# A gated recurrence and two MoE matmuls: first chunks of four batches at once, and all later loads uncast on GpSimd's queue

## The chip, the cores and the metric

The kernel runs on one core of one Trainium2 chip. The metric is the device time of one execution in microseconds (us), as a median over several runs. The kernel before takes 190.9 us (190.21 to 191.94, three runs). A verdict of faster or slower needs a difference of over 2%. The span of a profile is a little shorter than the time of its run, by 1.6 to 3 us here.

The engines are PE (TensorE matmul), PEld (its weight loads), DVE (VectorE), ACT (ScalarE), POOL (GpSimd) and SP (SyncE). Each works through its own instructions in a fixed order: in this kernel every instruction is pinned in the order that a small planner in the kernel works out beforehand.

## The reference

```
state = zeros(B, H, D, D)                       # B, H, S, D = 4, 8, 768, 48
for t in range(S):
    state = alpha[:, :, t, :, None] * state + einsum('bhd,bhe->bhde', k[:, :, t], v[:, :, t])
    y[:, :, t] = einsum('bhd,bhde->bhe', q[:, :, t], state)
x = y.transpose(0, 2, 1, 3).reshape(3072, 384)
h = x @ w_in                                    # 384 x 2048
out = (max(h, 0) ** 2) @ w_out                  # 2048 x 384
```

The recurrence is done in 24 chunks of 128 tokens, six for each batch. Each chunk has a cumulative decay (logarithm, triangular matmul, exponentials), scores, a mask and a value product. The state goes from a chunk to the next of the same batch, and starts at zero in each batch. The finished tokens (x tiles) feed two large matmuls, MoE1 and MoE2, which are most of PE's work.

## The kernel before

The first four chunks belong to batch 0. Alpha and q of these come in rows of four tokens ("slots"), k and v chunk by chunk. Later chunks follow batch by batch. Alpha, q and k go over SyncE's queue (all but seven early loads, which GpSimd issues uncast); v goes over GpSimd's queue and is cast to bf16 by the transfer itself, after a one-column copy that holds it back until the previous k has landed.

```
srcs = [("at", alpha), ("qt", q), ("kt", k), ("vt", v)]
slot_srcs = {n: a[0, :, 0:4 * P, :].rearrange("h (p j) d -> p h (j d)", j=4) for n, a in srcs}
srcs = [(n, a.rearrange("b h (c p) d -> b c p h d", p=P)) for n, a in srcs]
...
def load_tile(nm):
    if nm == "vt":
        return loads.tile([P, H, D], BF16, name=nm, bufs=LBV)      # LBV = 6
    return loads.tile([P, H, D], FP32, name=nm)                    # LB = 5
...
        def ld(nm=nm, src=src):                                    # in add_loads
            if nm not in d:
                d[nm] = load_tile(nm)
            if nm == "vt" and after:
                pin(nc.gpsimd.tensor_copy(d[nm][:, 0, 0:1], after["kt"][:, 0, 0:1]))
            pin((nc.gpsimd if pool or nm == "vt" else nc.sync).dma_start(out=d[nm], in_=src[b, c]))
...
ld_at = [load_slots("at", i * H // 2, (i + 1) * H // 2) for i in range(2)]
ld_qt = [load_slots("qt", i * H // 2, (i + 1) * H // 2) for i in range(2)]
for s in range(NJ):
    add_loads(s, ("kt", "vt"), pool=s == NJ - 1)
four_slots(ld_at, ld_qt)
for s in range(NJ):
    add_chunk(s)
for x in "iiiioo4oo5":                   # i, o: parts of w_in and w_out, by GpSimd
    ...
for s in range(6, NT):
    add_loads(s, after=C[s - 1])
    add_chunk(s)
```

The planner (`plan.run`) sorts all operations by a modelled start, and they are then issued in that order on each engine.

## Time and profile before

| what | before |
|---|---|
| time, median | 190.9 us |
| span of the profile | 189.4 us |
| first MoE matmul starts | 22.50 us |
| last matmul ends | 186.3 us |
| PE busy | 180.2 us (95%) |
| POOL busy | 42.2 us (22%) |
| DMA packets | 94,280 |

The prediction below shows the stretches, the chain and the timeline that matter. One more view belongs here, because it is the one that answers directly after a change: PE's waits, by whom it waited for, in us in total, times and the longest. The largest of the kernel before:

```profile
PE bank L229 <- DVE kI_s L474: 2.1, 2, 1.4
```

And the stretch from the first MoE matmul to 60 us as one row (length, busy us of PE, PEld, DVE, ACT and POOL with their instructions, granted PE clock, DMA share, GB/s):

```profile
22.50:60.00 37.50, 37.33 (x448) 29.29 (x449) 26.38 (x56) 26.20 (x63) 10.52 (x17) 0.97 1.21 183
```

PE rests 0.17 us of these 37.50, and POOL is busy for little more than a quarter.

### The profile page before, as it was taken

Reading aid. Unit: us, or ns where it says so; the run is one execution under the profiler, and the core shown is the slowest. Engines: PE = TensorE matmul, PEld = TensorE weight load, DVE = VectorE, ACT = ScalarE, POOL = GpSimd, SP = SyncE. Lnnn points to the kernel's source line nnn. Section 1 sums busy time; section 2 is a strip of 40 time slices with the busy share of each in tenths; the row PEclk is TensorE's granted clock in tenths of the full one; section 3 lists DMA queues with packets and bytes.
Section 4 is the critical chain, followed back from the end, with each engine's and each line's share of the span. In section 5 each row is a group of like instructions: output and inputs, shape, how many; then the busy total and the mean of one; then the engine's idle time right before and its main releaser. Section 6 shows DMA issues by size and latency. Waiting matters only on the chain.

```text
span 189.4 us, 5215 instructions
## 1 busy us (share of the span) xinstructions
PE 180.2 (95%) x1999; PEld 137.1 (72%) x1999; DVE 132.3 (70%) x335; ACT 126.7 (67%) x346; POOL 42.2 (22%) x78
## 2 busy tenths in 40 slices
PE   7864999999999999999999999999999999999993
PEld 2553778866878887777777787787787787777773
DVE  3167946754899795897886886886886886944411
ACT  3763459926778886678588588488588586565630
POOL 8967335023122233222021031041000000000000
PEclk9998589999999999999999999999999999999999
DMA  5999999899999999999959739739011011011112
GB/s 177 238 165 203 204 223 211 125 183 147 183 191 185 206 180 173 201 153 188 218 130 142 166 84 124 170 87 126 0 45 43 3 42 45 6 37 45 42 42 83
DMA packets 94280, 24.71 MB, mean 130 GB/s; under 512 B 85216, under 2 KB 93920, under 8 KB 94256
## 3 DMA queue, kind: packets, MB, share of 16 engines
q1 hardware_dynamic: 64992, 17.45, 44.8%
q0 software_dynamic: 29120, 6.88, 37.5%
q8 instruction: 15, 0.25, 0.6%
q14 instruction: 9, 0.07, 0.1%
q10 hardware_dynamic: 144, 0.05, 0.1%
HBM read 25.17 MB, written 4.72 MB: 158 GB/s over the span
## 4 chain that ended last, share of the span: by engine, by line
PE 87%; DMA 5%; SPq 3%; ACT 1%; DVE 1%; issue 1%; ACTq 0%; DVEq 0%
PE bank L226 78%; PE bank L229 7%; DMA kt<-in_k_dram 5%; PE st L226 2%; SPq L339 2%; SPq L319 1%; ACT r L668 1%; DVE st L578 1%; DVE sm L533 1%; ACT sb L583 0%; ACT xn L220 0%; DVE ob L736 0%; ACT ob L736 0%; ACT L_s L442 0%; DVE kI_s L474 0%
## 5 line engine op out<-in xcount | busy, mean ns | idle before, releaser
L668 ACT ACTIVATE r<-bank 128x256 bf16<-128x256 f32 (+1 forms) x160 | 64.7, 429 | 29.6 <-PE bank L226 28.2
L226 PE MATMUL bank<-xT_big,w_in_b 128*128 128x256 bf16 (+1 forms) x624 | 80.0, 266 | 0.1
L226 PE MATMUL bank<-w_out_b,gT 128*128 128x384 bf16 (+1 forms) x400 | 74.7, 320 | 0.0
L226 PEld LDWEIGHTS <-w_in_b 128*128 128x128 bf16 x624 | 53.8, 98 | 9.7 <-issue 0.5
L675 DVE TENSOR_TENSOR gT<-r 128x256 bf16<-128x256 bf16 (+1 forms) x160 | 47.6, 315 | 16.0 <-ACT r L668 14.4
L226 PEld LDWEIGHTS <-gT 128*128 128x128 bf16 x400 | 37.9, 98 | 15.8
L533 DVE TENSOR_TENSOR sm<-bank,utri_b 128x512 bf16<-128x512 f32 x40 | 25.3, 683 | 2.6 <-PE bank L226 2.5
L339 POOL DMA_DIRECT2D vt<-in_v_dram x24 | 21.3, 888 | 7.9 <-POOL vt L338 6.1
L338 POOL CAST vt<-kt 128x1 bf16<-128x1 f32 x18 | 4.7, 263 | 64.6 <-PE bank L226 41.8
L471 DVE TENSOR_TENSOR qA_s<-qt,A 128x384 bf16<-128x384 f32 x20 | 11.1, 556 | 9.5 <-ACT A L458 8.6
L218 DVE COPY qkT<-bank 128x1024 bf16<-128x1024 bf16 x20 | 13.8, 688 | 4.9 <-PE bank L229 4.9
L474 DVE TENSOR_TENSOR kI_s<-kt,Ainv 128x384 bf16<-128x384 f32 x24 | 13.3, 556 | 3.1 <-DMA kt<-in_k_dram 2.6
L709 ACT COPY ob<-bank 128x384 f32<-128x384 f32 x21 | 10.1, 480 | 8.1 <-PE bank L226 8.1
L226 PEld LDWEIGHTS <-qkT 64*128 64x128 bf16 (+1 forms) x260 | 10.4, 97 | 5.9 <-issue 2.5
L220 ACT CAST xn<-bank 128x384 bf16<-128x384 f32 x23 | 10.9, 480 | 4.2 <-PE bank L226 3.8
L583 ACT CAST sb<-st 128x384 bf16<-128x384 f32 x20 | 9.6, 478 | 5.7 <-DVE st L578 5.7
L458 ACT ACTIVATE A<-bank 128x384 bf16<-128x384 f32 x20 | 9.9, 496 | 2.4 <-PE bank L226 2.4
L229 PE MATMUL bank<-ident_bf,kI_s 128*128 128x128 bf16 x96 | 9.5, 223 | 2.1 <-DVE kI_s L474 2.1
L578 DVE TENSOR_TENSOR st<-st,ae_s 128x384 f32<-128x384 f32 x20 | 11.1, 556 | 0.0
L442 ACT ACTIVATE L_s<-at 128x384 bf16<-128x384 f32 x20 | 10.4, 521 | 0.0
L462 ACT ACTIVATE Ainv<-bank 128x384 bf16<-128x384 f32 x20 | 10.2, 510 | 0.0
L229 PE MATMUL bank<-ident_bf,qA_s 128*128 128x128 bf16 x96 | 9.3, 219 | 0.8 <-DVE qA_s L407 0.7
(78 smaller groups left out, 162.1 us busy)
## 6 DMA issues: line engine op xcount, KB each, us to landing
out_dram<-ob SPq DMA_DIRECT2D x23, 192.0 KB, 2.7
kt<-in_k_dram SPq DMA_DIRECT2D x21, 192.0 KB, 5.3
at<-in_alpha_dram SPq DMA_DIRECT2D x18, 192.0 KB, 4.8
qt<-in_q_dram SPq DMA_DIRECT2D x18, 192.0 KB, 4.7
vt<-in_v_dram POOLq DMA_DIRECT2D x24, 96.0 KB, 5.6
w_in_b<-in_moe_w_in_dram POOLq DMA_DIRECT2D x4, 384.0 KB, 11.0
w_out_b<-in_moe_w_out_dram POOLq DMA_DIRECT2D x4, 384.0 KB, 12.3
slot_at<-in_alpha_dram SPq DMA_DIRECT2D x2, 384.0 KB, 3.6
```

The source lines that it names most:

```text
L218: pin(nc.vector.tensor_copy(out, in_))
L220: pin(nc.scalar.copy(out, in_))
L226: pin(nc.tensor.matmul(*a, **kw))
L229: pin(nc.tensor.transpose(*a))
L339: pin((nc.gpsimd if pool or nm == "vt" else nc.sync).dma_start(out=d[nm], in_=src[b, c]))
L442: pin(nc.scalar.activation(L[:, :, 0:D], d["at"], AF.Ln))
L471: pin(nc.vector.tensor_mul(qA[:, :, 0:D], d["qt"], d["A"]))
L474: pin((nc.vector if mk.eng == "DVE" else nc.gpsimd).tensor_mul(kI[:, :, 0:D], d["kt"], d["Ai"]))
L533: pin(nc.vector.tensor_mul(d["sm"][:, hh], d["sc"][hh], (utri_p if first else utri_b).to_broadcast([P, NP, P])))
L578: pin(nc.vector.tensor_mul(st4, st4, bcast(ae, D)))
L668: pin(nc.scalar.activation(box["r"], box["ph"], AF.Relu))
L675: pin(nc.vector.tensor_mul(gT[g][:, f0:f0 + nf, 0:n], box["r"], box["r"]))
```

## The change

Its intent: the first chunk of every batch needs no incoming state, so the first chunks of all four batches are done together, by head pairs, with alpha, q and k in rows of four tokens, in parts of 96 KB. After that the chunks go batch by batch. All later loads, alpha, q, k and v, are issued by GpSimd without a cast, and a copy on GpSimd casts v to bf16. This gives fewer and larger packets and frees SyncE. A hold makes w_in wait for v's first part.

```diff
-    LB = 5
-    LBV = 6
+    LB = 4
+    SEQ = [(b, 0) for b in range(B)] + [(b, c) for b in range(B) for c in range(1, NCH)]
...
+    def load(s, names=("at", "qt", "kt", "vt")):
+        b, c = SEQ[s]
+        for nm in names:
+            def ld(nm=nm):
+                C[s][nm] = loads.tile([P, H, D], FP32, name=nm)
+                pin(nc.gpsimd.dma_start(out=C[s][nm], in_=srcs[nm][c, :, b * H:(b + 1) * H]))
+            C[s]["ld_" + nm] = pool_dma(LDS, X_ISSUE, ld, C[s - LB]["use_" + nm] if s - LB >= B else None)
...
+        def e_vb():
+            d["vb"] = work.tile([P, H, D], BF16, name="vb", bufs=4)
+            pin(nc.gpsimd.tensor_copy(d["vb"], d["vt"]))
+        if first:
+            vb = d["vb_op"]
+        else:
+            vb = d["use_vt"] = add("POOL", 0.52, e_vb, d["ld_vt"], C[s - 4].get("end") if s >= 8 else None, prio=-60.0)
...
+    ld_at = [load_part("at", h, nc.sync if h % 2 == 0 else nc.scalar, 0.9 + 0.45 * (h // 2)) for h in range(H)]
+    w_gate[:] = [bmask]
+    ld_qt = [load_part("qt", h, nc.sync, 2.7 + 0.45 * h) for h in range(B)]
+    ld_kt = [load_part_pool("kt", h) for h in range(B)]
+    ld_qt += [load_part("qt", h, nc.sync, 2.7 + 0.45 * h) for h in range(B, H)]
+    ld_kt += [load_part("kt", h, nc.sync, 4.5 + 0.45 * h) for h in range(B, H)]
...
+    ld_vt = [load_v(j, 8.1 + 0.45 * j) for j in range(NJ)]
+    def hold():
+        pin(nc.gpsimd.tensor_copy(w_in_b[0:PQ, 0, 0:1], v_0[0:PQ, 0, 0, 0:1]))
+    w_gate[:] = [add("POOL", 0.1, hold, ld_vt[0], utri, prio=-70.0)]
+    first_chunks(ld_at, ld_qt, ld_kt, ld_vt)
...
-    for s in range(6, NT):
-        add_loads(s, after=C[s - 1])
-        add_chunk(s)
+    order = ["i", "i", "i", "i", 4, "o", "o", "o", "o"]
+    for x in order + list(range(5, NT)):
+        ...
+            load(x)
+            if c == 1:
+                add_keys(b, 20.0 if b == 0 else 30.0)
+                add_state(b)
+            add_chunk(x)
```

Cut from the diff: the new masks, the first chunks' decay, transposes and copies by head pairs, the table of priorities, and the output of the first tiles in four-token rows.

## The prediction

> **What bounds the kernel now.** I read the page first, then busy time by stretch, then the chain of waits in order of time, then the timeline of the ramp. The page says PE 95% busy; by stretch:
>
> ```profile
> 0.00:6.00 6.00, 4.28 (x19) 1.87 (x20) 1.83 (x10) 2.83 (x3) 5.28 (x22) 1.00 0.67 193
> 6.00:14.00 8.00, 6.28 (x84) 4.17 (x83) 3.75 (x8) 5.63 (x15) 6.63 (x9) 1.00 1.65 195
> 14.00:22.50 8.50, 6.06 (x76) 4.14 (x71) 6.87 (x13) 3.89 (x10) 4.54 (x6) 0.73 1.28 202
> 22.50:36.00 13.50, 13.50 (x129) 11.35 (x130) 8.23 (x19) 10.12 (x20) 4.80 (x6) 0.92 1.32 208
> 36.00:60.00 24.00, 23.83 (x322) 17.94 (x320) 18.15 (x38) 16.08 (x44) 5.73 (x11) 1.00 1.15 170
> 60.00:160.00 100.00, 100.00 (x1137) 77.76 (x1135) 80.84 (x210) 74.75 (x222) 15.27 (x26) 1.00 0.80 122
> ```
>
> Columns: stretch, length, then PE, weight load, DVE, ACT, POOL busy (instructions), granted clock, DMA share, GB/s. From 22.5 us on PE never rests: that part is PE work alone, and a faster load there buys nothing. Only the ramp before 22.5 us, the lowered clock around it and a few gaps before 60 us can be gained. The chain of waits says what the ramp waits for:
>
> ```profile
> 3.47 2.81 SPq L339
> 6.33 9.01 DMA kt<-in_k_dram
> 22.50 15.27 PE bank L226 x139
> ```
>
> A key load is issued late, because SyncE's queue is held for 2.81 us, and takes 9.01 us. The timeline shows whom it holds, and what the first MoE matmul then waits for:
>
> ```profile
> 15.36 0.56 DVE L474 TENSOR_TENSOR kI_s<-kt,Ainv 128x384 bf16<-128x384 f32 x1 [1.69 <-DMA kt<-in_k_dram]
> 15.84 0.56 DVE L578 TENSOR_TENSOR st<-st,ae_s 128x384 f32<-128x384 f32 x1
> 16.31 1.28 DVE L533 TENSOR_TENSOR sm<-bank,utri_p 128x512 bf16<-128x512 f32 x2
> 22.50 0.80 PE L226 MATMUL bank<-xT_big,w_in_b 128*128 128x256 bf16 x3
> ```
>
> DVE runs in order, so the late key holds the state and mask multiplies behind it, and these hold the first tiles of x. MoE starts at 22.50 us; the last matmul ends at 186.3.
>
> **What the Trainium skill says.**
> 1. "DMA: Bandwidth & Descriptors", Specifications: transfers under 512 B miss line rate. The trace agrees: while the slot loads of alpha (768 B runs) flow alone, between 3 and 5 us, the row shows 330 to 390 GB/s; in 60 to 80 us, with runs of 192 B, 185.
> 2. The same page, "SWDGE vs HWDGE vs iDMA": GpSimd's descriptors are grouped into packets of up to 4 KB. The trace fits, for uncast loads only. Of the 29,120 packets on q0, the 24 cast loads of v take 24 x 1024 = 24,576 and the eight weight loads 4 x 384 + 4 x 512 = 3,584; 960 remain for seven uncast loads that have 7,168 runs of 192 B.
> 3. "SBUF — State Buffer", "SBUF: two separate sides": a GpSimd operation and a DVE operation with two SBUF inputs exclude each other for the whole instruction. The casts on GpSimd that the change adds could meet the squares. In this trace GpSimd's one-column casts take 0.18 to 0.57 us, which may be that; nothing here settles it.
> 4. "TensorE: Matmul & The Clock Gate", Part 1: PE's clock halves after a quiet window and returns after about 3.4 us of activity. The page of the kernel before shows the clock at 5 tenths in the slice around 19 to 24 us, after the sparse ramp.
>
> **The change part by part.**
>
> *Later loads, all on GpSimd's queue, uncast.* Before, in 60 to 80 us, a hardware packet cost 0.882 x 16 x 20 us / 14,256 = 19.8 ns and a packet of the casting v load 0.473 x 16 x 20 / 5,200 = 29.1 ns, so a cast load costs more DMA time than an uncast one of twice the written bytes. The change frees DMA time there, but PE is at 100.00 of 100: worth 0 us. Its cost: 4 issues x 0.88 us + one cast of some 0.5 us (estimate) = 4.0 us of GpSimd per chunk; PE takes about 164/24 = 6.8 us per chunk. It fits.
>
> *PE's work.* I counted matmuls in both orders and priced them by start-to-start times of the timeline (MoE1 66 in 7.22 us = 0.109; MoE2 8 in 1.30 = 0.163; transpose 8 in 0.45 = 0.056; state or inter-chunk 4 in 0.17 = 0.042; value product about 0.025). After the first MoE matmul the changed kernel has 16 more transposes (keys turned back, +0.90), 16 more state products (+0.68), 4 more inter-chunk products (+0.17), 3 fewer transposes of xn (-0.17), 8 fewer value products (-0.20): **+1.4 us**. Less lies before it (first chunks without states), but there PE waits anyway.
>
> *The ramp.* Four first chunks of four batches need no state, and all of alpha, q and k now comes in runs of 768 B. Step by step:
> - Alpha: 384 KB issued at 0.81 was in at 4.13. A part has 96 KB; less 0.8 us of transfer at 350 GB/s it lands about 2.5 us after issue. SyncE issues one per 0.46 us. ACT issues the other four; if its table load (0.80 to 2.08) holds that queue, heads 0 to 3 are in at about 5.1 us, if not, at 3.8. Half each.
> - ACT then does 4 logarithms x 0.52 + 8 exponentials x 0.50 + 2 small x 0.18 + one copy 0.59 = 7.0 us before the last inverse decay: 12.1 or 10.8.
> - Key multiply 0.56, transposes 0.3, copy 0.59, first scores and latency about 1: masks start near 14.6 or 13.3. All scores wait for all transposed heads.
> - DVE has six masks x 0.68, a copy 0.36, a mask 0.68, a copy 0.36 = 5.5 us before the first two x tiles are complete: 20.1 or 18.8, plus some 0.5 of latencies and stretch: 20.6 or 19.3. Middle **20.0, so -2.5 us** against 22.50.
> - Does v come in time? SyncE has issued 16 parts by about 8.2 us; 768 KB of v at 185 GB/s takes 4.2, with w_in beside it: landed about 15.5. Then four casts at 0.5 us: 16 to 18 us. The first value product needs its masks at about 16: close, not behind.
> - w_in is held back for v's first part, landing near 12: issued 12 to 15 us, the first part in at about 17.5, where it also is now (issue 8.85, plus 8.7). In time.
>
> *The sum.* -2.5 + 1.4 = -1.1 us, and a further -0.2 because the chunk loads are no longer pacing 40 to 60 us: 190.9 - 1.3 = **189.6 us**. The gain is small because the work in front of PE moves from waiting for k to a dense ACT and DVE line that ends only 2.5 us sooner.
>
> **The rivals.**
> - *ACT becomes the bound after the ramp.* From the start of MoE to the end of the first MoE1 rounds its order holds 20 relus x 0.60, 3 key copies, 2 chunks of decay work (2 x 1.9), 2 state casts, one xn: about 19 us, against about 19 us of PE work there (MoE1 of five tiles 13, MoE2 2.6, chunk 4 and keys 3). Three PSUM banks feed ACT, so lateness goes to PE at once. For: ACT had 10.12 of 13.50 us there before. It would give back 1 to 3 us: 190.6 to 192.
> - *GpSimd's line becomes the bound.* It does masks, four k parts, a hold, weights, casts and all loads in order. If v lands after 18 us, casts, w_out and chunk 4 all slip: up to +3 us, about 192.5. For: q0 waits in the trace for earlier transfers (1.0 to 1.6 us before several issues). Against: merged packets, and chunk 4 is first needed about 6 us into MoE.
> - *The clock.* Before, MoE's first 2.5 us ran at half clock, about 1.25 us lost. If the changed ramp keeps PE warm, 1.2 us more are gained: 188.4. Sparse transposes between 9 and 14 us speak against it.
> - *Everything goes well*: ACT's queue isn't held, the clock is up, and the gaps go (matmuls counted after 22.5 are 160.4 us of the 163.8 spent): 19.3 + 161.8 + 3.1 of tail + 1.6 between span and time = about 186.
>
> **Range and chances.** The start of MoE is uncertain by 1.3 us either way, what ACT or GpSimd gives back by 0 to 3, the clock by 1.2. The range is 186.5 to 192.4. Faster by 2% means under 187.1, which needs nearly all of the good case: 0.18. Slower by 2% means over 194.7, which needs loads late for several chunks: 0.07. Within 2%: 0.75.
>
> **What would show it.** Right: the wait for k gone from the chain, its place taken by ACT's exponentials and DVE's masks; first MoE matmul between 19 and 21 us; PE at 100 of 100 from 60 to 160 us as before; GpSimd busy near 50%; q0 with few, large packets. Wrong: PE gaps after 22 us that end with a relu (ACT), or with a load or value cast (GpSimd); a first MoE matmul after 22 or before 18.5 us; or a vanished dip of the clock, which would make the gain larger than the ramp's.

## The result, and the profile after

| what | before | after |
|---|---|---|
| time, median (four runs each) | 190.73 us | 199.57 us (198.55 to 199.91) |
| ratio of the fast runs | 1 | 1.0446, 95% interval 1.0383 to 1.0509 |
| span of the profile | 189.4 us | 196.7 us |
| first MoE matmul starts | 22.50 us | 21.65 us |
| last matmul ends | 186.3 us | 193.6 us |
| PE busy | 180.2 us (95%) | 181.5 us (92%) |
| POOL busy | 42.2 us (22%) | 95.2 us (48%) |
| DMA packets | 94,280 | 20,026 |

The changed kernel is slower by 4.5%. Here and below a ratio is the mean time of one kernel's fast runs over the mean of the other's fast runs of the same rounds, so it is not quite the ratio of the medians.

MoE starts 0.85 us earlier, and all of the loss comes after. PE's largest wait and the same stretch as before, now of the changed kernel, show where:

```profile
PE st L205 <- POOL vb L495: 5.1, 2, 4.2
```

```profile
22.50:60.00 37.50, 32.00 (x356) 24.58 (x354) 21.75 (x47) 22.20 (x53) 30.20 (x38) 0.90 1.09 217
```

The first row is a wait that did not exist before: a state matmul (`st`) waits for the cast of v (`vb`, L495) on GpSimd, twice, once for 4.2 us. The last row answers the one shown of before: PE rests 5.50 us of 37.50 in place of 0.17, and its clock is 0.90 in place of 0.97. GpSimd is busy three times as long.

GpSimd's timeline between 31 and 49 us (start, length, engine, line, operation, and in brackets the idle time before it and its releaser):

```profile
31.77 0.88 POOL L444 DMA_DIRECT2D vt<-in_v_dram  x1 [1.47 <-DMA vt<-in_v_dram]
32.65 0.52 POOL L495 CAST vb<-vt 128x384 bf16<-128x384 f32 x1
33.09 0.88 POOL L444 DMA_DIRECT2D at<-in_alpha_dram  x1
34.98 0.88 POOL L444 DMA_DIRECT2D qt<-in_q_dram  x1 [1.00 <-DMA w_out_b<-in_moe_w_out_dram]
36.92 0.88 POOL L444 DMA_DIRECT2D kt<-in_k_dram  x1 [1.06 <-DMA w_out_b<-in_moe_w_out_dram]
39.47 0.89 POOL L444 DMA_DIRECT2D vt<-in_v_dram  x1 [1.67 <-DMA w_out_b<-in_moe_w_out_dram]
...
47.46 0.88 POOL L444 DMA_DIRECT2D at<-in_alpha_dram  x1
48.34 0.52 POOL L495 CAST vb<-vt 128x384 bf16<-128x384 f32 x1
```

The load of v for chunk 5 is issued at 31.77 us. Its cast comes at 48.34 us. The row at 32.65 us is the cast of chunk 4; between the two casts stand thirteen issues, the loads of chunks 6, 7 and 8 and the alpha of chunk 9. That is 13 x 0.88 = 11.4 us of issuing and another 3.7 us in which three of these issues waited for parts of w_out to land. The order is fixed, so a cast of 0.52 us stands behind issues whose data nobody needs yet. Its own data had landed some 6 us before (at 42.23 us by the trace; put earlier, in the first experiment, the same cast waited for them to 42.24 us), and PE wanted the result at 44.7 us. A likely reason for the order lies in the planner, in the kernel above: it counts 0.88 us for an issue and knows nothing of these waits for earlier transfers, so its times for GpSimd and for the landing need not be those of the chip. No run tests that.

PE's side of it, and then the two stretches around it in the form of the rows above:

```profile
48.91 0.48 PE L205 MATMUL st<-vb,kI_s 128*128 128x96 bf16 x4 [4.21 <-POOL vb L495]
```

```profile
44.53:48.91 4.38, 0.17 (x3) 0.00 (x1) 0.24 (x1) 0.00 (x0) 4.26 (x7) 0.75 1.04 220
48.91:53.48 4.57, 4.57 (x38) 2.84 (x37) 2.79 (x5) 1.47 (x5) 4.57 (x6) 0.50 1.03 217
```

PE, DVE and ACT all stop for 4.4 us while only GpSimd issues loads. When the cast is done, PE works at half clock (0.50) for another 4.6 us. From 60 us on PE is full again in both kernels.

How the loss adds up: by the prediction's count and prices of matmuls (an estimate), PE has 160.4 us of work from the first MoE matmul on before, and 161.8 us after; it took 163.8 us before (22.50 to 186.3) and 171.95 us after (21.65 to 193.6). What is left over, 3.4 us before and 10.2 us after, is put down to gaps and clock: -0.85 (ramp) + 1.4 (more work) + 6.8 (gaps and clock) = +7.3 us, which is the difference of the spans, 196.7 - 189.4.

The ramp gained 0.85 us and not 2.5. Three engines' rows of the changed kernel, ACT, DVE and PE, and SyncE's largest wait in its issues, show what it waits for:

```profile
8.23 0.52 ACT L355 ACTIVATE L_f<-slot_at 128x384 bf16<-128x384 f32 x1 [2.53 <-DMA slot_at<-in_alpha_dram]
12.67 0.49 ACT L372 ACTIVATE Ainv<-bank 128x384 bf16<-128x384 f32 x1
...
10.18 1.03 DVE L375 TENSOR_TENSOR qk_f<-slot_qt,A 128x384 bf16<-128x384 f32 x2 [7.25 <-DMA slot_qt<-in_q_dram]
16.26 3.68 DVE L586 TENSOR_TENSOR sm<-bank,utri_p 128x512 bf16<-128x512 f32 x6 [1.08 <-PE bank L205]
...
21.65 0.85 PE L205 MATMUL bank<-xT_big,w_in_b 128*128 128x256 bf16 x3
```

```profile
SPq L328 <- DMA slot_at<-in_alpha_dram: 2.1, 3, 1.2
```

ACT stops for 2.53 us in the middle of its line because alpha's second half lands only at 8.2 us; the last inverse decay ends at 13.16 us, and the masks start at 16.26 us. SyncE's issues of q had to wait for earlier alpha parts to land (2.1 us), and so had ACT's last issue of alpha: it began only at 3.48 us, when the first part had landed. These waits fit the program's own semaphores: in every profile here the transfers of SyncE and ACT share eight semaphores and those of GpSimd have eight more, and no issue begins before the transfer that last used its semaphore has landed. Up to 15 transfers were under way at once, so a limit of the chip is not shown.

### The profile page after: what moved, and what is told of

Its sections match the earlier page's. It is cut to its first block, busy times and chain, and to the rows that moved or that the text cites. A ratio compares the mean times of both kernels' runs of the same rounds, so it can differ in the third digit from the quotient of the medians.

```text
span 196.7 us, 5302 instructions
## 1 busy us (share of the span) xinstructions
PE 181.5 (92%) x2011; PEld 138.1 (70%) x2012; DVE 134.0 (68%) x337; ACT 128.5 (65%) x350; POOL 95.2 (48%) x138
## 2 busy tenths in 40 slices
DMA packets 20026, 27.08 MB, mean 138 GB/s; under 512 B 6817, under 2 KB 16097, under 8 KB 20001
## 3 DMA queue, kind: packets, MB, share of 16 engines
q1 hardware_dynamic: 10256, 7.03, 13.3%
## 4 chain that ended last, share of the span: by engine, by line
PE 74%; DMA 17%; POOL 4%; issue 3%; SPq 1%; DVE 0%; ACT 0%
PE bank L205 66%; DMA w_out_b<-in_moe_w_out_dram 6%; PE bank L208 6%; DMA w_in_b<-in_moe_w_in_dram 5%; DMA slot_qt<-in_q_dram 3%; DMA v<-in_v_dram 2%; PE st L205 2%; DMA slot_at<-in_alpha_dram 2%; POOL w_in_b L266 1%; SPq L328 1%; POOL at L444 1%; POOL vt L444 1%; POOL qt L444 1%; POOL kt L444 1%; POOL vb L495 0%
## 5 line engine op out<-in xcount | busy, mean ns | idle before, releaser
L205 PE MATMUL bank<-w_out_b,gT 128*128 128x384 bf16 (+1 forms) x400 | 76.0, 323 | 0.0
L702 DVE TENSOR_TENSOR gT<-r 128x256 bf16<-128x256 bf16 (+1 forms) x160 | 49.0, 326 | 19.2 <-ACT r L695 17.8
L444 POOL DMA_DIRECT2D qt<-in_q_dram x20 | 17.7, 884 | 33.5 <-DVE gT L702 19.6
L586 DVE TENSOR_TENSOR sm<-bank,utri_b 128x512 bf16<-128x512 f32 x40 | 25.3, 683 | 2.4 <-PE bank L205 2.4
L444 POOL DMA_DIRECT2D vt<-in_v_dram x20 | 17.7, 885 | 3.3 <-DMA w_out_b<-in_moe_w_out_dram 1.7
L444 POOL DMA_DIRECT2D kt<-in_k_dram x20 | 17.7, 884 | 1.7 <-DMA w_out_b<-in_moe_w_out_dram 1.1
L444 POOL DMA_DIRECT2D at<-in_alpha_dram x20 | 17.7, 885 | 0.1
L526 DVE TENSOR_TENSOR qA_s<-qt,A 128x384 bf16<-128x384 f32 x20 | 11.4, 570 | 8.3 <-ACT A L513 7.5
L495 POOL CAST vb<-vt 128x384 bf16<-128x384 f32 x20 | 10.8, 541 | 5.6 <-PE bank L205 5.6
L205 PEld LDWEIGHTS <-qkT 64*128 64x128 bf16 (+1 forms) x240 | 10.2, 97 | 4.6 <-issue 3.2
L469 DVE TENSOR_TENSOR st<-st,ae_s 128x384 f32<-128x384 f32 x16 | 8.9, 558 | 5.9 <-PE st L205 5.9
L529 DVE TENSOR_TENSOR kI_s<-kt,Ainv 128x384 bf16<-128x384 f32 x20 | 11.1, 555 | 0.9 <-ACT Ainv L517 0.8
L205 PE MATMUL st<-vb,kI_s 128*128 128x96 bf16 x64 | 5.5, 209 | 5.1 <-POOL vb L495 5.1
```

The costliest lines, as they stand in the source:

```text
L205: pin(nc.tensor.matmul(*a, **kw))
L444: pin(nc.gpsimd.dma_start(out=C[s][nm], in_=srcs[nm][c, :, b * H:(b + 1) * H]))
L495: pin(nc.gpsimd.tensor_copy(d["vb"], d["vt"]))
L526: pin(nc.vector.tensor_mul(qA[:, :, 0:D], d["qt"], d["A"]))
L529: pin(nc.vector.tensor_mul(kI[:, :, 0:D], d["kt"], d["Ai"]))
L586: pin(nc.vector.tensor_mul(d["sm"][:, hh], d["sc"][hh], (utri_p if first else utri_b).to_broadcast([P, NP, P])))
```

## The experiments

### One cast moved: ahead of the burst, and further behind it

Theory: the place of the cast in GpSimd's order is the loss. Rival: the uncast loads themselves, or the added casts on GpSimd, are too slow. Both first runs change only the place of chunk 5's cast (the planner's order is edited after it is worked out).

```diff
     plan.run(gate)
...
+    def issue(s, nm):
+        return C[s]["ld_" + nm].deps[0]
+    move(C[5]["use_vt"], issue(7, "at"))       # first run: cast just before chunk 7's loads
+    move(issue(9, "qt"), C[5]["use_vt"])       # second run, instead: two more issues before it
+    move(issue(9, "kt"), C[5]["use_vt"])
+    plan.order.sort(key=lambda o: o.start)
```

> Chunk 5's cast of v stands nine load issues earlier in GpSimd's line, right after chunk 6's loads; nothing else moves. Theory (the cast's place in the in-order line): its data is in by then (issued at 31.8 us, such loads land in some 6 us), so the cast ends at about 41 us, the PE gap of 4.4 us before chunk 5's state goes, and with it the stretch of 4.6 us at clock 0.50, which cost about 2.1 us: 199.6 - 6.4 = about 193 us. Rival A (the load of v itself lands late, the cast only shows it): the cast now waits in its place for the load, PE still waits 2 us or more, time above 196. Rival B (ACT and DVE are overloaded between 22 and 60 us): the gap moves to a relu, time above 197.

> The opposite dose: two more load issues (chunk 9's q and k) stand before chunk 5's cast of v. Theory: PE's gap grows by 2 x 0.88 = 1.8 us to about 6.1 us, the half-clock stretch stays as long: about 201.3 us. Rival A or B: no change, 199.6 us.

Measured: 200.72 us with the cast early (ratio 1.0497) and 200.43 us with it late (1.0489). GpSimd and PE in the run with chunk 5's cast early, and as the last row PE in the run with it late:

```profile
42.24 0.69 POOL L495 CAST vb<-vt 128x384 bf16<-128x384 f32 x1 [1.89 <-DMA vt<-in_v_dram]
...
54.23 0.52 POOL L495 CAST vb<-vt 128x384 bf16<-128x384 f32 x1
...
44.74 0.33 PE L205 MATMUL st<-vb,kI_s 128*128 128x96 bf16 x4
...
54.80 0.48 PE L205 MATMUL st<-vb,kI_s 128*128 128x96 bf16 x4 [5.94 <-POOL vb L495]
```

```profile
51.19 0.48 PE L205 MATMUL st<-vb,kI_s 128*128 128x96 bf16 x4 [5.94 <-POOL vb L495]
```

The first time was a miss by 7.7 us, and a useful one. Chunk 5's gap was gone (its state matmul ran at 44.74 us), but now chunk 6's cast stood behind thirteen issues, and PE waited 5.94 us for it. In the changed kernel that cast came at 52.28 us, only 2 us sooner, and PE did not wait for it, because PE had already been stopped by the cast before. A single late cast hides the next. With two more issues in front of chunk 5's cast its gap grew from 4.21 to 5.94 us, by 1.73, which is 2 x 0.88 as expected, but the time grew by only 0.9 us (medians of different rounds; 1.8 us were expected). Where the rest went is not shown. The place of a cast sets the wait; that the whole loss hangs on it needed a kernel in which all casts are early.

### Cast by the transfer again, and all casts early

```diff
# cast by the transfer, as the kernel before did
-                C[s][nm] = loads.tile([P, H, D], FP32, name=nm)
+                if nm == "vt":
+                    C[s]["vb"] = C[s][nm] = loads.tile([P, H, D], BF16, name=nm, bufs=6)
+                else:
+                    C[s][nm] = loads.tile([P, H, D], FP32, name=nm)
...
-            vb = d["use_vt"] = add("POOL", 0.52, e_vb, d["ld_vt"], ...)
+            vb = d["ld_vt"]
```

> One part undone: the later loads of v are cast by the transfer again, as before the change, and GpSimd casts nothing after the first chunks; all loads stay on GpSimd's queue. Theory: no cast can stand behind load issues; both PE gaps (4.2 us at 48.9, 0.9 us at 33.2) and the slow clock go: about 192.3 us, if the dearer cast packets are hidden. Rival A (transfers late): the same or worse than 199.6 us.

```diff
# every cast from chunk 5 on ahead of the loads of two chunks later; bf16 buffers 4 to 6
+    for s in range(5, NT - 2):
+        if issue(s + 2, "at").start < C[s]["use_vt"].start:
+            move(C[s]["use_vt"], issue(s + 2, "at"))
```

> The earlier run with only chunk 5's cast moved gave 200.7 us: the gap of PE went over to chunk 6's cast (5.9 us, ended 54.2 us after twelve load issues). So now every cast of v from chunk 5 on stands right after the next chunk's loads, as chunk 4's did. Theory (any cast behind a burst of load issues): no gap over 1 us ends with a cast, no half-clock stretch after 30 us: 199.6 - 4.4 - 2.1 = about 193 us, near the 192.05 of casting in the transfer. Rival (GpSimd's line is too slow for issues and casts together, or the casts now hold up loads): a gap of PE remains that ends with a cast or a load, time above 196 us.

Measured: 192.05 us with the cast in the transfer, against 191.75 us of the kernel before in those rounds (ratio 1.0061, interval 0.9986 to 1.0135); 191.87 us with all casts early, against 191.29 us (1.0060, 1.0026 to 1.0094). The stretch from 22.5 to 60 us of the two, in this order, and GpSimd's casts in the second:

```profile
22.50:60.00 37.50, 37.07 (x469) 29.50 (x468) 27.27 (x58) 27.75 (x66) 30.48 (x36) 0.99 1.32 223
```

```profile
22.50:60.00 37.50, 36.21 (x461) 28.64 (x458) 27.27 (x57) 27.73 (x66) 28.94 (x37) 1.00 1.01 222
```

```profile
42.42 0.51 POOL L495 CAST vb<-vt 128x384 bf16<-128x384 f32 x1 [1.97 <-DMA vt<-in_v_dram]
46.37 0.52 POOL L495 CAST vb<-vt 128x384 bf16<-128x384 f32 x1
```

PE rests 0.43 and 1.29 us there, in place of 5.50, and the clock stays at 0.99 and 1.00. In the second run PE's wait for these casts is down from 5.1 to 0.2 us:

```profile
PE st L205 <- POOL vb L495: 0.2, 1, 0.2
```

The second run has the same uncast loads, the same casts and nearly the same busy time of GpSimd as the changed kernel; a cast simply comes every 4 us, once every four issues. (Its two more bf16 buffers are not the cause: in the changed kernel chunk 5's cast starts at the end of the issue before it, so it waited for no buffer.) It takes back 7.7 us (199.57 to 191.87 us, in different rounds). So the uncast loads and GpSimd's busy time cost no more than what is left of the ratio, 0.3 to 0.9% in the second run; the order cost the rest. The rival falls.

### How much of it is the clock

The gap is followed by half clock. Eighteen dummy matmuls of 512 columns just before chunk 5's state keep PE busy in the gap without doing anything.

```diff
+            if op is C[5]["ps_op"]:
+                dummies(18, op.start, op.start)
```

> 18 dummy matmuls of 512 columns (about 3.9 us) stand in the PE gap before chunk 5's state. The wait stays, only the clock should stay up. Theory (the gap also costs a half-clock stretch after it): the window 49 to 53 us keeps clock 1.00 and the time falls by about 2 us to 197.5. Against it: the clock falls anyway or the dummies end late, time 199.6 or more.

Measured: 196.71 us (ratio 1.0286), 2.9 us less than the changed kernel. PE in the gap, and the stretch after it:

```profile
44.58 4.05 PE L205 MATMUL bank<-warm 128*128 128x512 bf16 x17
49.40 0.33 PE L205 MATMUL st<-vb,kI_s 128*128 128x96 bf16 x4 [0.77 <-POOL vb L495]
```

```profile
49.40:53.97 4.57, 4.56 (x59) 3.28 (x59) 3.48 (x6) 2.41 (x7) 4.57 (x6) 1.00 1.02 219
```

The state matmul starts no earlier than in the changed kernel (49.40 and 48.91 us), but the clock is 1.00 behind it: the 4.57 us from it on hold 59 matmuls, where the same 4.57 us of the changed kernel, at 0.50, hold 38 (shown above). The 2.9 us of the medians may hold something else besides: the wait for chunk 4's cast did not occur in this profile. From that state matmul to the end of the span it took 145.9 us (195.3 - 49.40) in place of 147.8 (196.7 - 48.91), so the clock's after-effect is 2 to 3 us of the 7.7 (4.6 us of work at half speed would give 2.3). The rest, about 5 us, is the size of PE's two waits for casts, 4.21 and 0.94 us.

### Fewer, larger parts in the ramp

The ramp gained less than predicted. A first idea was that 24 small parts take too long to issue, and that 12 parts of 192 KB (all eight heads of a batch) would land sooner. It was tried on both repaired kernels.

```diff
-        return t[h % B * PQ:(h % B + 1) * PQ, h // B * B:(h // B + 1) * B]
+        return t[h * PQ:(h + 1) * PQ]
-    ld_at = [load_part("at", h, nc.sync if h % 2 == 0 else nc.scalar, ...) for h in range(H)]
+    ld_at = [load_part("at", b, nc.sync if b % 2 == 0 else nc.scalar, ...) for b in range(B)] * 2
```

> As the run before, and the first alpha, q and k loads in 12 parts of 192 KB in place of 24 of 96 KB. Theory ([...]small parts leave the DMA engines short): q's last part, landed at 9.3 us, comes 1 to 1.5 us sooner, v's first part 2 us sooner than 14.4, the first MoE matmul at 20.5 in place of 21.7 us: about 1 us less than the run before it. Rival (alpha, q and k aren't what the ramp ends with, DVE's masks are): no change over 0.5 us.

> Later v loads cast by the transfer, and the first loads in 12 parts of 192 KB. Theory: about 1 us less than with 24 parts (192.05 us), so 191.0, within 1% of the kernel before, which this set of loads can then just match. Rival (the size of the parts doesn't matter): 192 us.

Measured: 195.56 us (ratio 1.0236) and 195.18 us (1.0222, interval 1.0194 to 1.0250, so unclear at the limit of 2%), both more than 3 us worse than without it; the idea was wrong. In the chain of waits (start, length, what) alpha's first wait is this with the small parts (all casts early):

```profile
1.24 3.00 DMA slot_at<-in_alpha_dram
```

and with the large ones, where the first MoE matmul follows as the last row:

```profile
1.25 5.15 DMA slot_at<-in_alpha_dram
6.41 9.28 DMA v<-in_v_dram
```

```profile
24.57 0.75 PE L205 MATMUL bank<-xT_big,w_in_b 128*128 128x256 bf16 x3 [0.36 <-DVE xT_big L197]
```

With large parts no head is complete before all heads of all batches are, so the first logarithm waits to 7.14 us, where it began at about 4.8 us, and MoE starts at 24.57 us in place of 21.58 us. The small parts are what lets ACT begin at all. (ACT's operations of the ramp also come in another order, and the clock was low three times before 28.1 us, so the 3 us are not the size of the parts alone.)

### Is GpSimd's line the end of the ramp?

With all casts early, GpSimd issued four parts of w_in from 14.87 us and only then, at 17.95 us, cast the first v; PE waited 1.07 us for that. Two runs put the first casts between the second and third part of w_in, and the second of them gives two of the four casts to ACT, which is idle there.

```diff
+    for b in range(B):
+        C[b]["vb_op"].start = w_in_ready[2][0].deps[0].start - 1e-4 * (B - b)
# second run, in addition
+    for b in range(2):
+        C[b]["vb_op"].eng = "ACT"
```

> The changed kernel with every later cast of v early (191.87 us, first MoE matmul at 21.58 us), and in the ramp GpSimd's order w_in 0, w_in 1, the four first casts of v, w_in 2, w_in 3 in place of four w_in issues and then the casts. In the run with the casts early the first casts stood from 17.95 to 19.80 us behind four issues, PE waited 1.1 us for the first of them at 18.52 us, and w_in itself was the last wait (0.3 us) before the first MoE matmul. Theory 1 (GpSimd's line sets the end of the ramp): first value product near 17.6 us, first MoE matmul near 20.8 us, time some 0.7 us less, 191.2 us. Theory 2 (DVE's masks, 16.11 to 19.79 us, set it): first value product earlier but first MoE matmul still at 21.4 to 21.6 us, time 191.9 us.

> The same, and the first two casts of v on ScalarE, which stood idle from 15.4 to 18.9 us. Theory 1 (GpSimd's line): a further 0.3 us at most, first MoE matmul near 20.6 us. Theory 2 (DVE's masks): first MoE matmul still at 21.4 us or later, time 191.9 us. If both of these runs move the first MoE matmul and the time does not follow, the clock in 18 to 24 us is to be looked at.

Measured: 193.74 us (ratio 1.0142) and 191.61 us (1.0022, interval 0.9969 to 1.0075), against 191.39 us of the kernel before. PE in the first of them:

```profile
20.88 0.85 PE L205 MATMUL bank<-xT_big,w_in_b 128*128 128x256 bf16 x3
...
28.30 0.83 PE L205 MATMUL bank<-xT_big,w_in_b 128*128 128x256 bf16 x6 [0.57 <-DMA w_in_b<-in_moe_w_in_dram]
```

The first run did just what its theory said of the ramp: MoE began 0.7 us earlier, at 20.88 us. And the time rose by nearly 2 us (193.74 in place of 191.87, in different rounds): the later parts of w_in, now behind the casts, came too late, PE waited 0.9 us for them, and from about 20.6 to 24 us it ran at half clock. The second run has no such gap, but v landed later in it (GpSimd's first cast waited for it to 17.61 us, in place of 17.16), MoE began at 21.64 us, where it was, and PE, at half clock to 25 us, did not run into the end of w_in. Here the earlier start was worth nothing, because the next load was not there too. The second of these runs has the lowest ratio of the variants, but its interval tells it neither from the kernel before nor from the two repaired kernels (1.0061 and 1.0060). No version here beats the kernel before.

### What the ramp waits for

Two kernels with wrong results, built on the first of the last pair: the first chunks' q multiplies read alpha's slot, so DVE does not wait for q; in the second, q of the first chunks is not loaded either.

```diff
-                pin(nc.vector.tensor_mul(qk_f[:, i, p, ...], by_slot(nm), e[a]))
+                pin(nc.vector.tensor_mul(qk_f[:, i, p, ...], by_slot("at" if nm == "qt" else nm), e[a]))
# second kernel, in addition, in load_part
+            if nm != "qt":
                 pin(q.dma_start(out=slot_part(slot[nm], h), in_=row_part(nm, h)))
```

> Wrong results on purpose: the split order of the first run, and the first chunks' q multiplies read alpha's slot, so that DVE does not wait for q (7.05 us of waiting, to 9.98 us, in the run with the casts early); all loads run as before. Theory A (q's landing sets when DVE begins, and DVE's line of eight multiplies, copies and masks sets the end of the ramp): the first multiply starts near 8.5 us, masks start near 15.2 in place of 16.11 us, first MoE matmul 0.9 us earlier than in the first run. Theory B (the second half of q and k, or the exponentials, set the last multiply): masks start within 0.3 us of 16.1.

> Wrong results on purpose: as the kernel whose first q multiplies read alpha's slot (192.86 us, masks from 16.48 us, the third key multiply waiting for slot_kt until 13.22 us), and the eight parts of q are not loaded at all, so 768 KB fewer flow ahead of k's second half. Theory A (the ramp waits for its transfers, in order, so k's last parts land later by q's bytes or issues): the third key multiply starts near 11.6 us, no longer waits for slot_kt, masks start near 14.7 us, first MoE matmul near 20.3 us or at the landing of w_in. Theory B (ScalarE's line of exponentials and PE's transposes set it): masks start within 0.5 us of 16.5.

Each was run once: 192.86 us and 190.5 us. DVE in the first:

```profile
13.22 1.03 DVE L375 TENSOR_TENSOR qk_f<-slot_kt,Ainv 128x384 bf16<-128x384 f32 x2 [1.06 <-DMA slot_kt<-in_k_dram]
...
16.48 3.68 DVE L586 TENSOR_TENSOR sm<-bank,utri_p 128x512 bf16<-128x512 f32 x6 [1.56 <-PE bank L205]
```

and ACT and DVE in the second:

```profile
8.29 0.52 ACT L356 ACTIVATE L_f<-slot_at 128x384 bf16<-128x384 f32 x1 [2.55 <-DMA slot_at<-in_alpha_dram]
...
15.85 3.68 DVE L587 TENSOR_TENSOR sm<-bank,utri_p 128x512 bf16<-128x512 f32 x6 [1.08 <-PE bank L205]
```

DVE's 7 us wait for q is worth nothing by itself: without it DVE starts at 8.22 us, stops again for k until 13.22 us, and the masks start at 16.48 us. Without q's bytes the wait for k is gone, and still the masks start at 15.85 us, 0.6 us earlier, because alpha's second half lands at 8.3 us in this run, as in the changed kernel (it was 7.3 us in the run with q loaded; why it varies stays open), and ACT's line of exponentials follows from there. That is where the masks of the run that both are built on start, too (15.88 us), so neither kernel gained anything there. The reading: three loads, alpha's second half, q and k, end side by side, and taking one away shows the next. (The hold that waits for v's first part ran 3 us earlier without q, at 11.38 us in place of 14.26 us, and MoE began at 20.80 us in place of 21.68 us.)

### A warm ramp

The run with two casts on ACT had half clock from about 18.5 to 25.3 us. Ten dummy matmuls of 384 columns in two places where PE waited in the ramp should have kept the clock up.

```diff
+            n = 4 if op is C[2]["p2"] else 6 if op is C[0]["p3_op"] else 0
+            if n:
+                wp = ps_st.tile([P, NP, 2 * D], FP32, name="st").rearrange("p n j -> p (n j)")
+                for _ in range(n):
+                    mm(wp, lhsT=warm[:, 0:P], rhs=warm[:, 0:2 * NP * D], start=True, stop=True)
```

> The version with the first two casts of v on ScalarE and w_in issued in two halves (191.61 us), and ten 384-column matmuls of the constant tile on PE in two places of the ramp where it waited 0.80 us (for masks, near 16 us) and 1.08 us (for the first cast, near 17.5 us). Theory (the half clock at 18.7 to 24.7 us costs this version some 1.2 us of the MoE work after 21.6 us, and it comes of the sparse ramp): clock 1.00 in 20 to 24 us, first MoE matmul still at 21.6 us, nine MoE matmuls of the first group in 1.26 us in place of 2.10 us, time 190.4 us, some 1 us under the kernel before (191.4 us in those rounds). Rival (the clock falls in the ramp whatever PE is given there, or the ten matmuls delay the chain): clock still 0.50 in 20 to 24 us, time 191.6 us or more.

Measured: 192.28 us (ratio 1.0072, interval 1.0039 to 1.0105), 0.7 us more than without them; the rounds differ and the intervals overlap, so a loss is not shown, and the 1 us hoped for did not come. PE's dummies and its first MoE matmul:

```profile
16.51 1.46 PE L205 MATMUL st<-warm 128*128 128x384 bf16 x4
...
19.20 1.75 PE L205 MATMUL st<-warm 128*128 128x384 bf16 x6
...
23.01 0.49 PE L205 MATMUL bank<-xT_big,w_in_b 128*128 128x256 bf16 x3
```

In this execution the clock had already fallen before 14 us, so the dummies themselves ran at half clock, took 3.2 us where they were meant to fill 1.9, and delayed MoE to 23.01 us. The MoE work after that ran at full clock: three matmuls in 0.49 us in place of 0.85. The low clock was moved, not removed. In executions whose ramps differ little the low clock began at about 13.6, 18.5, 19.4 and 20.6 us. The traces show part of what sets the moment. Before the last matmuls, in all 14 profiles, a low stretch lasts 3.41, 6.83 or 10.24 us, once, twice or three times the same step, and all changes of one profile lie whole steps apart. Where this grid begins differs from one execution to the next: full clock comes first at 4.14 to 6.91 us, though PE's first matmul is at 1.25 or 1.26 us in every one. How little PE must do in a step for the clock to fall stays open.

## Why the prediction was wrong

It said 189.6 us, in a range of 186.5 to 192.4, with a chance of 0.07 for slower by over 2%. The time was 199.57 us. Its own list of signs had the right one: "PE gaps after 22 us that end ... with a load or value cast (GpSimd)".

- **"4 issues x 0.88 + one cast of some 0.5 us = 4.0 us of GpSimd per chunk; PE takes 6.8 us per chunk. It fits."** This is the step that failed. Its two durations were right: 0.88 us, and 0.52 us for the cast. What they add up to was right too: POOL is busy 48% of the span, as predicted. But a rate that fits on the average says nothing of when one instruction comes. The loads were free to run up to four chunks ahead, the order put thirteen of them in front of one cast, and three waited for w_out. The cast came 16.6 us after the issue of its load. The kernel with all casts early shows that the same work, evenly ordered, makes PE wait 0.2 us for casts in place of 5.1: 191.87 us. The thirteen issues between the casts of chunks 4 and 5 stand in the order of the instructions; the prediction used that order for counts, not for the distance between a producer and its consumer.
- **The rival "GpSimd's line becomes the bound"** was the right one, with the wrong place and size. It was tied to a late v of the first chunks and to chunk 4, "up to +3 us". The wait for chunk 4's cast was 0.94 us; chunk 5's was 4.21 us, at a point that the prediction did not consider, and the half clock behind it cost 2 to 3 us more. A stop of the bound engine was priced by its length alone.
- **The ramp, "-2.5 us"**, was -0.85. The term that was too small is the time to the masks: predicted at 14.6 or 13.3 us, measured at 16.26 us. The sum took one landing of alpha (5.1 or 3.8 us; the first logarithm began at 4.76 us) and then 7.0 us of ACT without a pause. ACT paused for 2.53 us for alpha's second half, whose last part was issued only at 3.48 us, and its last inverse decay ended at 13.16 in place of 12.1 or 10.8 us. From there to the masks it took 3.1 us, where the prediction had 2.5. From the masks to MoE the prediction had 6.0 us and the trace 5.4.
- **PE's work, "+1.4 us"**, is in agreement with the rest: the two kernels without the gap start MoE 0.8 and 0.9 us earlier than the kernel before, and their mean times are 0.6% longer. It was counted, and no run measures it alone.
- **ACT as the bound after the ramp** did not come: no relu is among PE's longer waits in the changed kernel or in those with early casts.
- **The later loads "worth 0 us"**: right, in the kernels where the casts come in time. PE is at 100 of 100 from 60 us to 160 us; with all casts early the transfers have 20,025 packets in place of 94,280, and none of that is in the time. The further -0.2 us for 40 to 60 us is smaller than these runs can tell.
- **The clock**, "1.2 us more" if PE stayed warm: PE's work of MoE ran at half clock for 2.2 us in the profile before (22.50 to 24.71) and for 1.15 us in the one after (21.65 to 22.80), some 0.5 us gained. As the grid of the clock lies elsewhere in each execution, that is partly luck.
- **The chain.** The wait for k is gone from it, as predicted; its place was to be taken by ACT's exponentials and DVE's masks, and was taken by transfers of alpha, q, v, w_in and w_out, and then by the burst of issues.
- **A reading that was off**: "between 3 and 5 us, the row shows 330 to 390 GB/s". That holds to about 4.4 us; from there to 5 us the row shows 209 to 289, still almost all in runs of 768 B. In the changed kernel alpha had less: 177 to 321 GB/s between 2 and 4 us in cells of 0.5 us.

The Trainium skill says in "TensorE: Matmul & The Clock Gate", Part 1, that the clock is judged in free-running windows of about 3.4 us: half clock after an idle window, and full clock after a busy one. The trace agrees on the windows: the clock falls at 46.69 us and rises at 53.52 us, 6.83 us or two steps of 3.41 later. It differs on "idle": the clock fell only 2.0 us after PE had stopped (44.70 us), and in the 3.41 us before the fall PE had been busy for 1.4 us.

## What to carry to other kernels

When compute and load issues share one in-order engine, the sum of their busy time tells little: look in the instruction order at what stands between each small producing instruction and the load it depends on, and put it ahead of every load that is not needed sooner. A stop of PE such as the one of 4.2 us here costs its length and the slow clock behind it (2 to 3 us), and it can hide the next late instruction, so a fix of one place should be made in all places of that kind. And a faster start is worth only what the next transfer in line allows.

## What the Trainium skill lacked or had wrong

- "DMA: Bandwidth & Descriptors", section "Issuing engines are not separate DMA queues", says that issuing from several engines saves only the time to initiate a transfer, which is usually small beside the transfer. On GpSimd here an uncast load of 192 KB took 0.88 us to issue (its landing some 4 us), and thirteen of them in a row, 11.4 us with 3.7 us of their own waits, made PE stop for 4.21 us. The passage does not warn that on an engine that also computes, an issue holds up the computing behind it.
- The same page, "Anatomy of one DMA — SWDGE (gpsimd) path", calls the descriptor generation small and variable. The trace does not part an issue into dispatch and descriptors, but as a whole it is not small for the issuing engine: 80 issues x 0.88 us = 71 of GpSimd's 95.2 busy us.
- "TensorE: Matmul & The Clock Gate", Part 1, puts the cost of the clock's ramp under 1% of a typical span. That is of a kernel's start; here a later gap of 4.21 us was followed by half clock worth 2 to 3 us, 1 to 1.5% of the time, and filling the gap with dummy matmuls took 2.9 us back (199.57 to 196.71 us). The page lets the moment of the change vary by 500 ns either way; in the 14 profiles here full clock first comes at 4.14 to 6.91 us, with PE's first matmul at 1.25 or 1.26 us in all of them.
- "SBUF — State Buffer", "SBUF: two separate sides": the exclusion of GpSimd and DVE hardly showed as a cost of the casts. Their median was 0.515 us with a longest of 0.812, while DVE was busy two thirds of the time. Whether the longer ones are that exclusion, no run tests.
- No page that was read tells how many transfers may be under way before an issue waits. Here SyncE's issues of the first q parts waited 2.1 us in all for earlier parts of alpha to land; by the trace they ended when one of the program's eight semaphores came free, and with up to 15 transfers under way no limit of the chip showed.
